# GpSimd's operations behind attention go to VectorE, and the planner gets new costs

## The chip, the cores and the metric

One core of a Trainium2 chip runs the whole program in one launch. The engines are TensorE (PE, matmuls; PEld is its weight load), VectorE (DVE), ScalarE (ACT), GpSimd (POOL) and SyncE (SP, which issues the DMAs). The metric is the device time of one execution in microseconds. The kernel before took 591.49 us, the median of three runs (590.26 to 592.46).

## The reference

Three stages follow one another. The first is a decayed linear attention over 2 batches, 8 heads, 768 tokens and 64 columns per head, in blocks with a running state; its output is one matrix of 1536 tokens x 512. Two feed-forward layers follow, 512 to 2048 to 512:

```python
x = attn_out.transpose(0, 2, 1, 3).reshape(B * S, H * D)        # 1536 x 512
h = x @ w_in;  g = where(h > 0, h, exp(min(h, 0)) - 1);  x = g @ w_out       # layer 0, ELU
h = x @ w_in2; g = maximum(h, 0) + log1p(exp(-abs(h)));  y = g @ w_out2      # layer 1, softplus
```

All data is float32.

## The kernel before, in words

**Numbers in two parts.** Each float32 matrix is split into a high part (rounded by ScalarE to the matmul's format) and a low part (value minus high part, a `tensor_tensor` subtract). A product is three matmuls: high x high, high x low, low x high (L387 to L389 for `x @ w_in`, L437 for `g @ w_out`). All large matmuls have 512 columns.

**Tiles.** The 1536 tokens are three tiles t = 0, 1, 2 of 512. The 2048 hidden columns of a layer are 16 blocks c of 128. A key (layer, t, c) is one block of hidden values for one tile: 12 matmuls into a PSUM bank (`hps`), the activation on ScalarE and VectorE, a split into g (high on ScalarE, L777, low by `minus`, L545), and 12 matmuls into the four accumulators y0 to y3. When a run of keys of one tile (a unit) ends, the four accumulators are taken out to `yacc` (L1094 and L1096 copy, L1099 adds), and the next unit's y matmuls wait for that.

**PLAN.** "one" runs a block for tile 0, "two" a pair of blocks for tiles 1 and 2, and "fast" (layer 0 only, seven pairs) does a pair of blocks for tiles 1 and 2 with 7 half products instead of 8; in exchange it needs sums and differences of blocks of x (`first_sums`, L996 on, tiles `sums`, t1 to t4) and of weights (`sum_ops`, L830 on, tiles `sumsw`, s0 and s1). These are elementwise operations between SBUF tiles; `minus` is L545, `plus` L548. The products go to PSUM tiles pa, pb and pd; `copy_op` (L936 ScalarE, L938 VectorE) and `add_op` (L945) combine them. ELU ends in L450; softplus ends in L758 (s5), `minus` (s6) and L764 (s7), which also gives the PSUM bank back. There are four such banks (b0 to b3).

**Weights** arrive as 64-bit words; ScalarE (L628, L632) and VectorE (L637, L642) make floats of them, ScalarE the high part (L647), `minus` the low one. SP loads them.

**The order.** Attention with the first eight blocks is written out by hand (`start`, `early_step`), with GpSimd doing some of it (L273, L279, L377, L1282). Everything behind it is made of `Op` objects in `build()`: `on` says on which engines an operation may run and what it is thought to cost, `key` is its due time, `after` its predecessors. `schedule()` plays this through at build time: whenever an engine falls free in the plan, it takes the ready operation with the earliest due time, and that emits the instruction. On the chip each engine then runs its own list strictly in order. An operation that may run on either engine (`both`, `half`) goes to the one that the plan finds free first; V_LO, W_LO, W_SUM, W_HALF, W_SLO, T_LO, T_SUM and SOFT are such. The plan's costs are MM3 for three matmuls, SCALAR for ScalarE, TT_V and TT_G for an operation with all operands in SBUF on VectorE and GpSimd, PS_V for one that reads PSUM; `both and pool[0] > now` stretches a VectorE operation that the plan sees beside a GpSimd one. PE picks between y matmuls (`m2_seq`) and products (`m1_seq`); at PILE = 2 ready keys the y matmuls come first.

**The end.** The last unit's four accumulators are added, stored by SP in four DMAs, and `probe()` (L1223) runs 15 matmuls into a free bank.

Of the kernel before, what the change touches and what calls it, by code (L numbers as in the profile page):

```python
# [55 lines left out]
def body(ctx, tc, lamc, attqk, attkv, w1, w2, out):  # L56
# [398 lines left out]
    order = count()  # L455

    class Op:

        def __init__(self, on, key, fn, after=(), gate=None, end=None):
            self.on, self.key, self.fn, self.gate, self.done = on, key, fn, gate, end  # L460
            self.then, self.wait, self.n, self.gone, self.first = [], 0, next(order), False, False
            self.behind(*after)
            ops.append(self)
# [7 lines left out]
    def schedule(pe, free):  # L471
# [3 lines left out]
        heads = [0] * len(pe)  # L475
        pool = [0.0]

# [6 lines left out]
        def begin(op, e):  # L484
            op.gone = True
            took = op.on[e]
            if e == "V" and isinstance(took, tuple):
                took, both = took
                if both and pool[0] > now:
                    over = pool[0] - now  # L490
                    took = over + took - SHARE * over if SHARE * over < took else took / SHARE
            if e == "G":
                pool[0] = now + took
            op.fn(e) if len(op.on) > 1 else op.fn()
            busy, late = took if isinstance(took, tuple) else (took, took)
            free[e] = now + busy
            heappush(events, (free[e], next(seen), None))
            heappush(events, (now + late + 0.06, next(seen), op))
# [5 lines left out]
        while left:  # L504
            now, _, op = heappop(events)
            if op is not None:
                left -= 1
                if op.done:
                    op.done()
                for nxt in op.then:  # L510
                    nxt.wait -= 1
                    if nxt.wait == 0:
                        enter(nxt)
            if events and events[0][0] <= now:
                continue
            if free["P"] <= now:
                m2_seq, m1_seq = pe
                ahead = list(takewhile(lambda o: o.wait == 0, m2_seq[heads[0]:heads[0] + 8]))
                can = [bool(ahead), heads[1] < len(m1_seq) and m1_seq[heads[1]].wait == 0]
                can[1] = can[1] and (m1_seq[heads[1]].gate is None or m1_seq[heads[1]].gate())  # L520
                if can[0] and (not can[1] or sum(o.on["P"] > MM3 for o in ahead) + sum(o.on["P"] == MM3 for o in ahead) // 4 >= PILE and not m1_seq[heads[1]].first):
                    pick = 0
                else:
                    pick = 1 if can[1] else None
                if pick is not None:
                    heads[pick] += 1
                    begin(pe[pick][heads[pick] - 1], "P")
            for e in "SAGV":
                if free[e] > now:
                    continue  # L530
                ready[e] = [x for x in ready[e] if not x[2].gone]
                for x in ready[e]:
                    if x[2].gate is None or x[2].gate():
                        begin(x[2], e)
                        break
            if not events and left:
                raise RuntimeError(f"stuck: {left}, {[(q[h].key, q[h].wait) for q, h in zip(pe, heads) if h < len(q)]}")
        return now


    MM3, SCALAR, TT_V, TT_G, PS_V = 0.68, 0.65, (0.71, True), 1.4, (0.71, False)
    SHARE, PILE = 0.35, 2

# [6 lines left out]
    engines = {"V": V, "G": G}  # L550
    both = {"G": TT_G, "V": TT_V}
    half = {"G": 0.76, "V": (0.42, True)}
    wide = {"G": 2.7, "V": (1.28, True)}

    def build():
# [54 lines left out]
        def weights_ops():  # L610
            for k, task in enumerate(tasks):
# [45 lines left out]
                o2 = Op({"A": SCALAR}, key, a2, [o1, summed_[t1] if t1 else None])  # L657
                o3 = Op({"V": 0.55}, key, v1, [o1])
                o4 = Op({"V": 0.75}, key, v2, [o3, o2])
                o5 = Op({"A": SCALAR}, key, a3, [o4])  # L660
                o6 = Op(W_LO, key, v3, [o5])
                loads[task] = ld, o2
# [40 lines left out]
        for key in queue[EARLY - 2:]:  # L703
            pos = nom["m2", key]
            if begins(key) or ends(key):
                parts = [Op({"P": MM3}, pos + m * MM3, lambda key=key, m=m: m2_part(key, m)) for m in range(KD)]
            else:
                parts = [Op({"P": 4 * MM3}, pos, lambda key=key: m2(key))]
            m2_ops[key], m2_last[key] = parts, parts[-1]
            m2_seq.extend(parts)  # L710
            for p in parts:
                p.behind(need(("o", key[0] * NF + key[2])))

        def act_ops(key, src, after, done):

# [3 lines left out]
            if layer == 0:  # L719
# [12 lines left out]
                o = Op({"A": SCALAR}, k, x2, [o])  # L732
                o = Op({"V": PS_V}, k, x3, [o], end=done)
            else:
# [33 lines left out]
                o = Op({"A": SCALAR}, k, s2, [o])  # L768
                o = Op(PLUS_ONE, k, s3, [o])
                o4 = Op({"A": SCALAR}, k, s4, [o])  # L770
                o5 = Op({"V": PS_V}, k, s5, [o4])
                o6 = Op(SOFT, k, s6, [o5], end=lambda: eu.append(box["i"]))
                o = Op({"V": PS_V}, k, s7, [o6], end=done)

# [9 lines left out]
            h = Op({"A": SCALAR}, k, hi, [o, m2_last.get(queue[j - 3])])  # L784
            low = Op(V_LO, k, lo, [h], end=lambda: vfree.add(box["k"]))
            for p in m2_ops[key]:
# [43 lines left out]
        def sum_ops(q):  # L830
# [26 lines left out]

            o0 = Op(W_SUM, k0, g0, deps)
            o1 = Op(W_HALF, k0, g1, deps)
            o2 = Op(W_HALF, k0, g2, deps)  # L860
            o3 = Op(W_HALF, k0, lambda e: plus(e, cut(0), cut(3), cut(0)), [o1, o2])
            o4 = Op(W_HALF, k1, lambda e: minus(e, cut(3), cut(1), cut(3)), [o0, o3])
            o5 = Op(W_HALF, k0, lambda e: minus(e, cut(1), cut(0), cut(1)), [o4])
            o6 = Op(W_HALF, k1, lambda e: minus(e, cut(2), cut(2), cut(1)), [o5])
            out_ = []
            for i, key, deps in ((0, k0, [o5, o3]), (1, k1, [o6, o4])):
# [9 lines left out]
                h = Op({"A": SCALAR}, key, hi, deps + held.get(("s", i), []))  # L876
                out_.append(Op(W_SLO, key, lo, [h]))
            held["sums_r"] = out_
# [4 lines left out]
        def quick(layer, p):  # L883
# [47 lines left out]
            def copy_op(src, tag, key, after):  # L931
# [7 lines left out]

                return Op(COPY, key, fn, after + held.get(tag, []))  # L940

# [23 lines left out]
            held["s", 0], held["s", 1] = [p5, p6], [p3, p7]  # L965
            held["p1"] = [act_ops(keys[0, 1], lambda: box["p1"], [a11], None)]
            held["u2"] = [act_ops(keys[0, 2], lambda: box["u2"], [a12], None)]
            held["p5"] = [act_ops(keys[1, 2], lambda: box["p5"], [a22], None)]
            act_ops(keys[1, 1], lambda: box["a"], [p4], lambda: give_bank(box["a"]))
# [12 lines left out]
        def part_ops(i, k, f, key, deps, new):  # L982
# [10 lines left out]
            h = Op({"A": SCALAR}, key, hi, deps)  # L993
            return h, Op(T_LO, key, lo, [h])

        def first_sums(plain_end):  # L996
# [10 lines left out]
            def chain(name, key, deps, *terms):  # L1007
                o = None
                for i, (fn, a, b) in enumerate(terms):

                    def go(e, i=i, fn=fn, a=a, b=b):
                        fn(e, box[name], a() if a else box[name], b())

                    o = Op(T_SUM, key, go, deps if o is None else [o])
                return o
# [61 lines left out]
        def unit_ops(u):  # L1077
# [8 lines left out]
            for m in range(KD):  # L1086
# [15 lines left out]
                if fresh:  # L1102
# [3 lines left out]
                    if layer == 0 and t == 2:  # L1106
                        deps += [gone["i", 0], gone["i", 1]]
                o = Op(COPY if fresh else {"V": PS_V}, key, fn, deps)
                mine.append(o)
# [14 lines left out]
        def split_ops(t):  # L1124
# [4 lines left out]
            for m in range(KD):  # L1129
# [10 lines left out]
                prev = h if m == 0 else prev  # L1140
                xdone[1, t].append(Op(V_LO, key0 + m * MM3 - 3.0, lo, [h]))
            held["acc", t] = list(xdone[1, t])


# [12 lines left out]
        def close_units(keys_done):  # L1157
            while made_units[0] < len(units) and all(k in keys_done or queue.index(k) < EARLY for k in units[made_units[0]]):
# [4 lines left out]
                if t in ysplit and (1, t) not in xdone:  # L1163
                    split_ops(t)

# [35 lines left out]
    NV = 9  # L1201
    W_LO = both
    V_LO = both
    W_SUM, W_HALF, W_SLO = both, half, both
    T_LO, T_SUM = both, both
    SOFT = both
    PLUS_ONE = {"A": SCALAR}
# [3 lines left out]
    def close_attention():  # L1211
# [3 lines left out]
        late["tp"] = ctx.enter_context(tc.tile_pool(name="ltp", bufs=1, reuse_waits="tile"))  # L1215

    def probe():
        ps = pp.tile([P, TT], F32, tag="b0", name="probe")
        a, x = halves["i", 2 * NF - 1][0][:, 0:P], xh[0][0]
        b = x.rearrange("p a n -> p (a n)")  # L1220
        for n in (256, 384, 512):
            for i in range(5):
                T.matmul(ps[:, :n], a, b[:, :n], start=True, stop=True, skip_group_check=True)  # L1223

# [72 lines left out]
    with tc.manual_schedule():  # L1297
# [4 lines left out]
        build()  # L1302
        probe()

# [45 lines left out]
```

## Time and profile before

| | |
|---|---|
| median of three runs | 591.49 us |
| the profiled execution | 590.46 us |
| its span, first to last instruction | 588.7 us |
| mean granted clock of TensorE | 0.994 |
| PE busy | 573.4 us (97%) |
| DVE busy | 414.9 us (70%) |
| ACT busy | 368.4 us (63%) |
| POOL busy | 316.7 us (54%) |

Shares are of the span. A matmul is recorded from its start to its modelled end, and matmuls overlap, so PE's speed is read from the distance of their starts. The list of waits says how long an engine stood idle and whose work ended the wait. A granted clock of 1 is 2.4 GHz, of 0.5 it is 1.2 GHz.

### The profile page before, as it was taken

How to read it: one execution, taken by the hardware profiler on the slowest of the kernel's cores; microseconds unless marked ns; L12 is line 12 of the kernel's file. 1: busy time of each engine (PE TensorE's matmuls, PEld its weight loads, DVE VectorE, ACT ScalarE, POOL GpSimd, SP SyncE). 2: the span in 40 equal slices, each digit the busy share in tenths (PEclk: the TensorE clock that was granted, in tenths of full speed). 3: DMA queues.
4: the chain of work that ended last, by engine and by line, in shares of the span. 5: the costliest groups of instructions: out<-in, count | busy, mean ns of one | idle time of the engine just before them, and what ended most of it. 6: DMA issues, size and time to landing. Idle time of an engine off the chain costs nothing.

```text
span 588.7 us, 8054 instructions
## 1 busy us (share of the span) xinstructions
PE 573.4 (97%) x2999; PEld 467.9 (79%) x2999; DVE 414.9 (70%) x546; ACT 368.4 (63%) x652; POOL 316.7 (54%) x246
## 2 busy tenths in 40 slices
PE   8899999979999989999999999999999999999999
PEld 7777778757788878888888788887888887888887
DVE  6678778999868398845887937687785479633732
ACT  1365657647876667645868568887794488464720
POOL 4634356998755374544374835547453555343541
PEclk9999999989999999999999999999999999999999
DMA  8944642101214122420223102132223011000023
GB/s 317 409 165 126 243 157 90 37 0 36 73 45 135 38 70 72 144 72 1 84 96 107 37 1 72 36 108 71 73 71 108 1 37 36 1 0 1 0 85 130
DMA packets 14582, 49.80 MB, mean 85 GB/s; under 512 B 1744, under 2 KB 1744, under 8 KB 14544
## 3 DMA queue, kind: packets, MB, share of 16 engines
q1 hardware_dynamic: 14544, 49.30, 24.3%
q8 instruction: 23, 0.38, 0.3%
q14 instruction: 15, 0.12, 0.1%
HBM read 46.14 MB, written 3.15 MB: 84 GB/s over the span
## 4 chain that ended last, share of the span: by engine, by line
PE 63%; DVE 20%; ACT 5%; DMA 5%; POOL 3%; issue 3%; SPq 0%; DVEq 0%; ACTq 0%
PE y L437 31%; PE hps L387 8%; PE hps L388 8%; PE hps L389 8%; DMA raw<-w 4%; DVE r L164 2%; PE pa L387 2%; PE pa L389 2%; PE pa L388 2%; DVE sums L545 2%; DVE u L758 2%; DVE v L450 2%; DVE r L642 2%; DVE r L637 2%; DVE yacc L1099 1%
## 5 line engine op out<-in xcount | busy, mean ns | idle before, releaser
L545 POOL TENSOR_TENSOR g<-v,g 128x512 fp32r<-128x512 f32 x69 | 96.1, 1393 | 98.2 <-ACT g L777 98.2
L437 PE MATMUL y<-g,woh 128*128 128x512 f32 x384 | 119.4, 392 | 0.8 <-ACT yacc L1094 0.8
L437 PE MATMUL y<-woh,g 128*128 128x512 f32 x384 | 118.2, 389 | 0.0
L777 ACT ACTIVATE g<-v 128x512 fp32r<-128x512 f32 x89 | 56.1, 631 | 73.7 <-PE y L437 68.6
L545 POOL TENSOR_TENSOR v<-v,u 128x512 f32<-128x512 f32 x38 | 52.9, 1392 | 61.7 <-DVE u L758 61.7
L437 PEld LDWEIGHTS y<-g,woh 128*128 128x128 f32 x384 | 71.6, 188 | 17.1 <-ACT yacc L1094 1.6
L437 PEld LDWEIGHTS y<-woh,g 128*128 128x128 f32 x384 | 72.1, 188 | 14.9
L387 PE MATMUL hps<-xh,wih 128*128 128x512 f32 x200 | 79.6, 398 | 0.8 <-DVE v L764 0.6
L388 PE MATMUL hps<-xl,wih 128*128 128x512 f32 x200 | 78.3, 391 | 0.4 <-POOL xl L545 0.4
L389 PE MATMUL hps<-xh,wil 128*128 128x512 f32 x200 | 78.1, 391 | 0.0
L437 PE MATMUL y<-g,wol 128*128 128x512 f32 x192 | 74.8, 389 | 0.0
L437 PE MATMUL y<-wol,g 128*128 128x512 f32 x192 | 74.7, 389 | 0.0
L1099 DVE TENSOR_TENSOR yacc<-y,yacc 128x512 f32<-128x512 f32 x68 | 45.4, 687 | 35.9 <-PE y L437 35.8
L758 DVE SCALAR_TENSOR_TENSOR u<-u,e 128x512 f32<-128x512 f32 x48 | 43.6, 908 | 32.4 <-ACT v L754 32.4
L642 DVE CUSTOM_DVE_ANT_0 r<-r,c 128x1024 uint16<-128x1024 uint16 x49 | 46.8, 956 | 6.7 <-ACT c L632 6.1
L387 PEld LDWEIGHTS hps<-xh,wih 128*128 128x128 f32 x200 | 37.8, 189 | 11.8 <-DVE v L764 2.7
L764 DVE SCALAR_TENSOR_TENSOR v<-hps,v 128x512 f32<-128x512 f32 x48 | 32.8, 684 | 18.2 <-POOL v L545 18.0
L388 PEld LDWEIGHTS hps<-xl,wih 128*128 128x128 f32 x200 | 37.8, 189 | 8.2 <-POOL xl L545 0.8
L389 PEld LDWEIGHTS hps<-xh,wil 128*128 128x128 f32 x200 | 37.7, 188 | 7.9
L437 PEld LDWEIGHTS y<-wol,g 128*128 128x128 f32 x192 | 36.0, 188 | 7.5
L437 PEld LDWEIGHTS y<-g,wol 128*128 128x128 f32 x192 | 36.0, 188 | 7.5
L741 ACT ACTIVATE e<-hps 128x512 f32<-128x512 f32 x48 | 28.2, 587 | 16.0 <-PE hps L389 15.0
(198 smaller groups left out, 1158.4 us busy)
## 6 DMA issues: line engine op xcount, KB each, us to landing
raw<-w SPq DMA_DIRECT2D x64, 512.0 KB, 3.7
qk<-attqk SPq DMA_DIRECT2D x8, 512.0 KB, 7.0
kv<-attkv SPq DMA_DIRECT2D x8, 512.0 KB, 7.0
out<-yacc SPq DMA_DIRECT2D x12, 256.0 KB, 2.1
early<-attkv SPq DMA_DIRECT2D x2, 512.0 KB, 9.2
early<-attqk SPq DMA_DIRECT2D x2, 512.0 KB, 10.6
earlykv<-attkv SPq DMA_DIRECT2D x2, 512.0 KB, 10.9
earlyqk<-attqk SPq DMA_DIRECT2D x2, 512.0 KB, 10.9
```

Of the source, the lines that this page charges most:

```text
L164: V.tensor_tensor(out=ri, in0=ri, in1=c, op=ALU.add)
L387: T.matmul(ps, wh[:, wo[i]], xa[i], start=(start and i == 0), stop=False, skip_group_check=True)
L388: T.matmul(ps, wh[:, wo[i]], xb[i], start=False, stop=False, skip_group_check=True)
L389: T.matmul(ps, wl[:, wo[i]], xa[i], start=False, stop=(stop and i == n - 1), skip_group_check=True)
L437: T.matmul(yps[m], a, b, start=(begins(key) and i == 0), stop=(ends(key) and i == 2))
L545: engines[e].tensor_tensor(out=o, in0=a, in1=b, op=ALU.subtract)
L642: V.tensor_tensor(out=ri, in0=ri, in1=box["c"], op=ALU.add)
L741: A.activation(out=box["e"], in_=src(), func=AF.Abs)
L758: V.scalar_tensor_tensor(out=u, in0=u, scalar=-1.0, in1=box["e"], op0=ALU.add, op1=ALU.subtract)
L764: V.scalar_tensor_tensor(out=box["v"], in0=src(), scalar=0.0, in1=box["v"], op0=ALU.max, op1=ALU.add)
L777: A.activation(out=g[:, 0], in_=box["v"], func=AF.Copy)
L1099: V.tensor_tensor(out=y, in0=yps[m], in1=y, op=ALU.add)
```

## The change

Every group that could go to either engine behind attention now has only VectorE in its dictionary. An operation that takes its engine as an argument is made by `Either`, since the number of engines no longer tells. In the planner's model, VectorE and GpSimd operations whose operands are all in SBUF would hold a common port one after the other (`port`); a GpSimd operation would start only with QUEUE ready ones waiting for VectorE; but no operation has GpSimd in its dictionary. New costs: VectorE 0.69 us (half size 0.415), ScalarE 0.635, and `PIPE`: the engine falls free that much before the result is there. The activation of keys of the fast pairs whose value lies in SBUF is marked as such (`bank=False`). The count of ready y matmuls is now a sum of their costs. `second_sums()` is the counterpart of `first_sums` for layer 1; it is called only where FAST[1] is true, and it is false. `probe()` and its call are gone. The hand-written attention part is as before.

```diff
+    def Either(on, key, fn, after=(), gate=None, end=None):
+        return Op(on, key, fn, after, gate, end, True)
...
-        pool = [0.0]
+        port = {"V": 0.0, "G": 0.0}
...
             took = op.on[e]
-            if e == "V" and isinstance(took, tuple):
-                took, both = took
-                if both and pool[0] > now:
-                    over = pool[0] - now
-                    took = over + took - SHARE * over if SHARE * over < took else took / SHARE
-            if e == "G":
-                pool[0] = now + took
-            op.fn(e) if len(op.on) > 1 else op.fn()
-            busy, late = took if isinstance(took, tuple) else (took, took)
+            op.fn(e) if op.names else op.fn()
+            if e in "VG":
+                took, shared = took
+                if shared:
+                    took += max(0.0, port["VG"[e == "V"]] - now - 0.14)
+                    port[e] = now + took
+            busy, late = took if isinstance(took, tuple) else (took - PIPE[e], took)
...
-                if can[0] and (not can[1] or sum(o.on["P"] > MM3 for o in ahead) + sum(o.on["P"] == MM3 for o in ahead) // 4 >= PILE and not m1_seq[heads[1]].first):
+                if can[0] and (not can[1] or sum(o.on["P"][0] for o in ahead) / (4 * MM3) >= PILE and not m1_seq[heads[1]].first):
...
+                if e == "G" and sum(not x[2].gone for x in ready["V"]) < QUEUE:
+                    continue
...
-    MM3, SCALAR, TT_V, TT_G, PS_V = 0.68, 0.65, (0.71, True), 1.4, (0.71, False)
-    SHARE, PILE = 0.35, 2
+    MM3, SCALAR, SB_V, SB_G, PS_V = 0.68, 0.635, (0.69, True), (1.295, True), (0.69, False)
+    PIPE = {"P": 0.0, "A": 0.1, "V": 0.08, "G": 0.04, "S": 0.0}
+    PILE, QUEUE = 2, 3
...
-                o3 = Op({"V": 0.55}, key, v1, [o1])
-                o4 = Op({"V": 0.75}, key, v2, [o3, o2])
+                o3 = Op({"V": (0.42, True)}, key, v1, [o1])
+                o4 = Op({"V": SB_V}, key, v2, [o3, o2])
                 o5 = Op({"A": SCALAR}, key, a3, [o4])
-                o6 = Op(W_LO, key, v3, [o5])
+                o6 = Either(W_LO, key, v3, [o5])
...
-    W_LO = both
-    V_LO = both
-    W_SUM, W_HALF, W_SLO = both, half, both
-    T_LO, T_SUM = both, both
-    SOFT = both
+    W_LO = {"V": SB_V}
+    V_LO = {"V": SB_V}
+    W_SUM, W_HALF, W_SLO = {"V": SB_V}, {"V": half["V"]}, {"V": SB_V}
+    T_LO, T_SUM = {"V": SB_V}, {"V": SB_V}
+    SOFT = {"V": SB_V}
     PLUS_ONE = {"A": SCALAR}
     COPY = {"A": SCALAR, "V": PS_V}
...
-    def probe():
-        ps = pp.tile([P, TT], F32, tag="b0", name="probe")
-        a, x = halves["i", 2 * NF - 1][0][:, 0:P], xh[0][0]
-        b = x.rearrange("p a n -> p (a n)")
-        for n in (256, 384, 512):
-            for i in range(5):
-                T.matmul(ps[:, :n], a, b[:, :n], start=True, stop=True, skip_group_check=True)
...
         build()
-        probe()
```

## Rows read from the trace of the kernel before

**Rows 1.** Windows: stretch, length, then busy us and count by engine, clock, DMA

```profile
95.20:584.90 489.70, 480.65 (x2098) 393.18 (x2097) 344.85 (x427) 320.51 (x567) 274.02 (x204) 1.00 0.17 56
...
93.40:124.80 31.40, 27.16 (x118) 21.50 (x116) 30.05 (x26) 17.80 (x33) 30.11 (x21) 1.00 0.14 46
93.40:159.90 66.50, 60.40 (x254) 47.88 (x253) 62.59 (x66) 43.65 (x79) 59.09 (x45) 0.97 0.14 46
204.90:216.90 12.00, 11.05 (x49) 8.82 (x47) 11.76 (x14) 7.34 (x14) 9.63 (x10) 1.00 0.30 107
126.30:129.70 3.40, 3.40 (x9) 2.63 (x9) 3.40 (x5) 1.54 (x3) 3.40 (x3) 0.51 0.00 0
```

**Rows 2.** Chain that ended last: start us, us, what, how many

```profile
554.29 30.60 PE y L437 x135
```

**Rows 3.** PE's waits from 100 us on: us in total, times, longest

```profile
PE pd L387 <- DVE v L450: 4.2, 1, 4.2
PE pa L387 <- DVE p L938: 1.7, 1, 1.7
PE pa L387 <- DVE p L945: 1.1, 2, 0.9
PE y L437 <- ACT yacc L1094: 0.8, 1, 0.8
PE hps L387 <- DVE v L764: 0.8, 2, 0.6
PE hps L388 <- POOL xl L545: 0.4, 1, 0.4
```

**Rows 4.** Timeline of PE behind its longest pause: start us, us, what

```profile
126.47 0.63 PE L387 MATMUL pd<-t1h,s0h 128*128 128x512 f32 x1
126.90 0.63 PE L388 MATMUL pd<-t1l,s0h 128*128 128x512 f32 x1
```

**Rows 5.** Timeline of DVE, the operation that ended the pause

```profile
124.81 0.68 DVE L450 SCALAR_TENSOR_TENSOR v<-v,hps 128x512 f32<-128x512 f32 x1
```

**Rows 6.** Timelines of DVE and POOL, working beside each other

```profile
118.07 1.77 DVE L545 TENSOR_TENSOR sums<-sums,xl2a 128x512 f32<-128x512 f32 x1
119.77 1.78 DVE L545 TENSOR_TENSOR sums<-xh,sums 128x512 f32<-128x512 f32 x1
...
117.56 1.74 POOL L545 TENSOR_TENSOR s1l<-sumsw,s1h 128x512 fp32r<-128x512 f32 x1
```

**Rows 7.** Timeline of DVE with POOL idle beside it

```profile
99.66 0.68 DVE L548 TENSOR_TENSOR sums<-sums,xl2a 128x512 f32<-128x512 f32 x1
100.26 0.68 DVE L545 TENSOR_TENSOR sums<-sums,xl 128x512 f32<-128x512 f32 x1
...
162.23 0.41 DVE L545 TENSOR_TENSOR sumsw<-sumsw 128x256 f32<-128x256 f32 x1
162.56 0.68 DVE L450 SCALAR_TENSOR_TENSOR v<-v,p 128x512 f32<-128x512 f32 x1
```

**Rows 8.** Timeline of ACT, a wait in front of the first evictions

```profile
116.50 0.63 ACT L870 ACTIVATE s1h<-sumsw 128x512 fp32r<-128x512 f32 x1 [1.05 <-DVE sumsw L545]
```

**Rows 9.** Groups by line: count, busy us, mean ns, idle before, releaser

```profile
L545 POOL TENSOR_TENSOR g<-v,g 128x512 fp32r<-128x512 f32 x69 | 96.1, 1393 | 98.2 <-ACT g L777 98.2
...
L1099 DVE TENSOR_TENSOR yacc<-y,yacc 128x512 f32<-128x512 f32 x68 | 45.4, 687 | 35.9 <-PE y L437 35.8
...
L1096 DVE COPY yacc<-y 128x512 f32<-128x512 f32 x11 | 7.6, 690 | 1.9 <-PE y L437 1.7
L1094 ACT ACTIVATE yacc<-y 128x512 f32<-128x512 f32 x13 | 7.5, 593 | 9.7 <-PE y L437 9.7
```

**Rows 10.** The end: chain, DMA issues by SP, and DMA landing times

```profile
584.89 2.62 PE probe L1223 x15
...
561.84 24.13 SPq L1114 DMA_DIRECT2D out<-yacc  x12
...
out<-yacc SPq DMA_DIRECT2D x12, 256.0 KB, 2.1
```

More of the change, by code (lines that the diff above doesn't have):

```diff
@@ L455, in body, with __init__ @@
     order = count()
+    def Either(on, key, fn, after=(), gate=None, end=None):
+        return Op(on, key, fn, after, gate, end, True)
     class Op:
-        def __init__(self, on, key, fn, after=(), gate=None, end=None):
+        def __init__(self, on, key, fn, after=(), gate=None, end=None, names=False):
             self.on, self.key, self.fn, self.gate, self.done = on, key, fn, gate, end
             self.then, self.wait, self.n, self.gone, self.first = [], 0, next(order), False, False
+            self.names = names
             self.behind(*after)
@@ L550, in body @@
     engines = {"V": V, "G": G}
-    both = {"G": TT_G, "V": TT_V}
-    half = {"G": 0.76, "V": (0.42, True)}
-    wide = {"G": 2.7, "V": (1.28, True)}
+    both = {"V": SB_V, "G": SB_G}
+    half = {"V": (0.415, True), "G": (0.74, True)}
     def build():
@@ L705, in build @@
             if begins(key) or ends(key):
-                parts = [Op({"P": MM3}, pos + m * MM3, lambda key=key, m=m: m2_part(key, m)) for m in range(KD)]
+                parts = [Op({"P": (MM3, MM3 + 0.17)}, pos + m * MM3, lambda key=key, m=m: m2_part(key, m)) for m in range(KD)]
             else:
-                parts = [Op({"P": 4 * MM3}, pos, lambda key=key: m2(key))]
+                parts = [Op({"P": (4 * MM3, 4 * MM3 + 0.17)}, pos, lambda key=key: m2(key))]
             m2_ops[key], m2_last[key] = parts, parts[-1]
@@ L712, in build, with act_ops @@
                 p.behind(need(("o", key[0] * NF + key[2])))
-        def act_ops(key, src, after, done):
+        def act_ops(key, src, after, done, bank=True):
             layer, t, c = key
@@ L732, in act_ops @@
                 o = Op({"A": SCALAR}, k, x2, [o])
-                o = Op({"V": PS_V}, k, x3, [o], end=done)
+                o = Op({"V": PS_V if bank else SB_V}, k, x3, [o], end=done)
             else:
@@ L768, in act_ops @@
                 o = Op({"A": SCALAR}, k, s2, [o])
-                o = Op(PLUS_ONE, k, s3, [o])
+                o = Either(PLUS_ONE, k, s3, [o])
                 o4 = Op({"A": SCALAR}, k, s4, [o])
-                o5 = Op({"V": PS_V}, k, s5, [o4])
-                o6 = Op(SOFT, k, s6, [o5], end=lambda: eu.append(box["i"]))
-                o = Op({"V": PS_V}, k, s7, [o6], end=done)
+                o5 = Op({"V": SB_V}, k, s5, [o4])
+                o6 = Either(SOFT, k, s6, [o5], end=lambda: eu.append(box["i"]))
+                o = Op({"V": PS_V if bank else SB_V}, k, s7, [o6], end=done)
             def hi():
@@ L784, in act_ops @@
             h = Op({"A": SCALAR}, k, hi, [o, m2_last.get(queue[j - 3])])
-            low = Op(V_LO, k, lo, [h], end=lambda: vfree.add(box["k"]))
+            low = Either(V_LO, k, lo, [h], end=lambda: vfree.add(box["k"]))
             for p in m2_ops[key]:
@@ L856, in g2 @@
                 plus(e, cut(0), f32(halves[tb][0][:, HALF:DM]), f32(halves[tb][1][:, HALF:DM]))
[L858 to L864, printed above, removed]
+            o0 = Either(W_SUM, k0, g0, deps)
+            o1 = Either(W_HALF, k0, g1, deps)
+            o2 = Either(W_HALF, k0, g2, deps)
+            o3 = Either(W_HALF, k0, lambda e: plus(e, cut(0), cut(3), cut(0)), [o1, o2])
+            o4 = Either(W_HALF, k1, lambda e: minus(e, cut(3), cut(1), cut(3)), [o0, o3])
+            o5 = Either(W_HALF, k0, lambda e: minus(e, cut(1), cut(0), cut(1)), [o4])
+            o6 = Either(W_HALF, k1, lambda e: minus(e, cut(2), cut(2), cut(1)), [o5])
             out_ = []
@@ L876, in sum_ops @@
                 h = Op({"A": SCALAR}, key, hi, deps + held.get(("s", i), []))
-                out_.append(Op(W_SLO, key, lo, [h]))
+                out_.append(Either(W_SLO, key, lo, [h]))
             held["sums_r"] = out_
@@ L938, in fn @@
                         V.tensor_copy(h, box[src])
-                return Op(COPY, key, fn, after + held.get(tag, []))
+                return Either(COPY, key, fn, after + held.get(tag, []))
             def add_op(tag, src, key, after, done=None):
@@ L965, in quick @@
             held["s", 0], held["s", 1] = [p5, p6], [p3, p7]
-            held["p1"] = [act_ops(keys[0, 1], lambda: box["p1"], [a11], None)]
-            held["u2"] = [act_ops(keys[0, 2], lambda: box["u2"], [a12], None)]
-            held["p5"] = [act_ops(keys[1, 2], lambda: box["p5"], [a22], None)]
+            held["p1"] = [act_ops(keys[0, 1], lambda: box["p1"], [a11], None, False)]
+            held["u2"] = [act_ops(keys[0, 2], lambda: box["u2"], [a12], None, False)]
+            held["p5"] = [act_ops(keys[1, 2], lambda: box["p5"], [a22], None, False)]
             act_ops(keys[1, 1], lambda: box["a"], [p4], lambda: give_bank(box["a"]))
@@ L993, in part_ops @@
             h = Op({"A": SCALAR}, key, hi, deps)
-            return h, Op(T_LO, key, lo, [h])
+            return h, Either(T_LO, key, lo, [h])
         def first_sums(plain_end):
@@ L1012, in go @@
                         fn(e, box[name], a() if a else box[name], b())
-                    o = Op(T_SUM, key, go, deps if o is None else [o])
+                    o = Either(T_SUM, key, go, deps if o is None else [o])
                 return o
@@ L1107, in unit_ops @@
                         deps += [gone["i", 0], gone["i", 1]]
-                o = Op(COPY if fresh else {"V": PS_V}, key, fn, deps)
+                o = Either(COPY if fresh else {"V": PS_V}, key, fn, deps)
                 mine.append(o)
@@ L1140, in split_ops, with second_sums, keep, hi @@
                 prev = h if m == 0 else prev
-                xdone[1, t].append(Op(V_LO, key0 + m * MM3 - 3.0, lo, [h]))
+                xdone[1, t].append(Either(V_LO, key0 + m * MM3 - 3.0, lo, [h]))
             held["acc", t] = list(xdone[1, t])
+        def second_sums():
+            p = next(p for kind, layer, p in PLAN if kind == "fast" and layer == 1)
+            pos = [nom[1, p, "P", k] - 3.0 for k in range(7)]
+            y = {(t, m): o for t in (1, 2) for m, o in enumerate(ysplit[t])}
+            clear = xuse[1] + xuse[2]
+            done = {i: [] for i in (1, 2, 3, 4)}
+            xdone[1, 1], xdone[1, 2] = [None] * KD, [None] * KD
+            made_x = {}
+            reads = {1: [], 2: []}
+            tmp = {}
+            prior = {}
+            def keep(t, m, key):
+                def hi():
+                    if t not in made_x:
+                        made_x[t] = True
+                        new_x(t, 1)
+                    A.activation(out=xh[t][m // 2][:, m % 2], in_=yacc[0, t][m], func=AF.Copy)
+                def lo(e):
+                    minus(e, xl[t][m // 2][:, m % 2], yacc[0, t][m], f32(xh[t][m // 2][:, m % 2]))
+                h = Op({"A": SCALAR}, key, hi, [y[t, m]] + clear)
+                o = Either(V_LO, key, lo, [h])
+                xdone[1, t][m] = o
+                reads[t].append(o)
+                return o
+            def sub(key, out_, a, b, deps):
+                return Either(V_LO, key, lambda e: minus(e, out_(), a(), b()), deps)
+            def yy(t, m):
+                return lambda: yacc[0, t][m]
+            for i in range(2):
+                def tmp_new(i=i):
+                    tmp[i] = late["hp"].tile([P, TT], F32, tag=("p1", "p5")[i], name="sums3")
+                k11 = keep(1, i, pos[0])
+                k21 = keep(1, 2 + i, pos[1])
+                k22 = keep(2, 2 + i, pos[3])
+                def t3(e, i=i, tmp_new=tmp_new):
+                    tmp_new()
+                    minus(e, tmp[i], yacc[0, 2][2 + i], yacc[0, 2][i])
+                f3 = Either(V_LO, pos[2], t3, [y[2, i], y[2, 2 + i]] + held.get(("p1", "p5")[i], []))
+                f1 = sub(pos[2], yy(2, i), yy(2, i), yy(1, i), [f3, y[1, i]])
+                f2 = sub(pos[3], yy(2, 2 + i), yy(2, 2 + i), yy(2, i), [f1, k22])
+                f4 = sub(pos[6], yy(1, 2 + i), yy(1, 2 + i), yy(2, 2 + i), [f2, k21])
+                for n, f, o in ((1, yy(2, i), f1), (2, yy(2, 2 + i), f2), (3, lambda i=i: tmp[i], f3), (4, yy(1, 2 + i), f4)):
+                    h, low = part_ops(n, i, f, pos[{1: 2, 2: 3, 3: 5, 4: 6}[n]], [o, prior.get(n)] + clear, i == 0)
+                    prior[n] = h
+                    done[n].append(low)
+                    if n == 3:
+                        held[("p1", "p5")[i]] = [low]
+                reads[2] += [f1, f2, done[1][-1], done[2][-1], f3]
+                reads[1] += [f1, f4, done[4][-1]]
+                reads[2] += [f4]
+            held["acc", 1], held["acc", 2] = reads[1], reads[2]
+            tdone[1] = done
@@ L1163, in close_units @@
                 if t in ysplit and (1, t) not in xdone:
-                    split_ops(t)
+                    if t == 0 or not FAST[1]:
+                        split_ops(t)
+                    elif t == 1:
+                        second_sums()
         keys_done = {k for k in queue[:EARLY]}
```

## Prediction

> **What bounds the kernel now.** I read the stretches first, by windows: from the end of the attention part to the last y matmul TensorE (PE) is busy 480.7 of 489.7 us, VectorE (DVE) 344.9, GpSimd (POOL) 274.0 [rows 1]. So a microsecond is won only where PE stands still or runs slowly. Next, how much that is: in the chain of work 135 matmuls behind one another take 30.60 us, 0.2267 us each [rows 2]; the stretch has 2098 of them [rows 1], and 2098 x 0.2267 = 475.6. About 14.1 us are lost, the most that the change can win. The list of PE's waits names 9.0 of them [rows 3]; the largest, 4.2 us, is one wait of pd for a DVE operation of L450. The timeline of PE shows the price behind it: after that pause the matmuls start 0.43 us apart [rows 4], and the granted clock of that stretch is 0.51, the 1.2 GHz level [rows 1]. Eight such steps cost 8 x 0.20 = 1.6 us. The rest, some 3.5 us, is slips of 0.1 to 0.3 us.
>
> Why was L450 as late as 124.81 [rows 5]? Before it DVE and POOL worked on the block sums side by side, and the reader should see how: DVE starts at 118.07 and 119.77, 1.70 us apart, one POOL operation beside each, and all of them are recorded at over 1.7 us [rows 6]. Where nothing of POOL's runs beside it, a 128x512 operation of DVE lets the next start after 0.60 us (99.66, 100.26) and a 128x256 one after 0.33 (162.23, 162.56) [rows 7]; below I take 0.605 and 0.335. So a lockstep pair of large ones costs 1.70 us, and the same two on DVE alone 1.21: this is the whole argument for the change.
>
> **The change part by part.** *All of POOL's work behind attention to DVE.* From 95.2 to 584.9 DVE has 427 operations and POOL 204 [rows 1]. At 0.605 us each (the half-size ones too, an upper price) 631 take 382 us of 489.7, 78%. DVE's busy time now is 344.9, although its own 427 cost at most 258 alone: the lockstep stretches them by 87 us, and that is given back. DVE has room over the whole; the question is the places.
>
> *The first sums, 93.4 to 124.8.* DVE has 26 operations there, POOL 21 [rows 1]; one of each had begun before. 45 x 0.605 = 27.2 us; nine are of half size (as the short one in [rows 7]), which takes 9 x 0.27 off: 24.8. In the same order L450 would start at 93.4 + 24.8 to 27.2 = 118.2 to 120.6 instead of 124.81: 4.2 to 6.6 us earlier. The wait was 4.2, so it goes (-4.2), and with it the slow clock behind it (-1.6). The 0.8 us wait for yacc on ScalarE [rows 3] lies in the same stretch: ScalarE's queue stood behind a 1.05 us wait for a sumsw of DVE [rows 8], which falls earlier with the rest (-0.8). What is late next: pd needs a free bank, the t1 and the s12 halves; all three are in the count.
>
> *The second knot, 204.9 to 216.9.* PE waits 1.7 us for a copy of L938 [rows 3]. DVE had 14 operations, POOL 10, in the 12 us [rows 1]: 24 x 0.605 = 14.5 at the upper price; with seven half-size ones, and without the three at the edges, which need not be done first, 21 x 0.605 - 7 x 0.27 = 10.8. That is 1.2 us earlier than now or, at the upper price, 2.5 later. The half-size price is the measured one; I take -1.0.
>
> *Layer 2.* Waits of 0.8 us in two places for L764, and 0.4 for an xl of POOL [rows 3]. The operations ahead of them are stretched ones; bounds 0 and -1.2, I take -0.8. The 1.1 us for p of L945 stay: the matmul needs an addition that needs the matmul before it.
>
> *Low part of g.* It ran on POOL 69 times, 1393 ns on the mean [rows 9]; on DVE alone an operation of this size is done in 0.7 [rows 7]. The chain from ScalarE's high part to the y matmul gets 0.7 us shorter wherever DVE is free. PE has other matmuls ready then: 0.
>
> *New waits.* DVE's queue runs in order, so what POOL did beside it now stands in front of something. The tightest stage is 93.4 to 159.9: 66 and 45 operations [rows 1], two of them begun before; 109 x 0.605 = 65.9, with 29 half-size ones 58.1, for a stage that would shrink from 66.5 to 59.9 us (-4.2 - 1.6 - 0.8). That is 97% or more of it. Weight preparation, which is not urgent, can move past the stage; bounds of the loss 0 and the whole 6.6, I take +1.0, nearer to 0 because the lateness that was measured already has these operations in it.
>
> *The schedule's new costs.* DVE 0.69 with the next start 0.08 earlier, ScalarE 0.635 with 0.1 earlier, are for DVE what the rows show [rows 7]; before, it planned 0.71 without overlap and shared stretches of another form. This alters the order in ways that no row gives: bounds -3.5 (all slips gone) and +3.5, I take 0. Names, the unused second_sums and the evened count of ready matmuls: 0.
>
> *The probe.* Its 15 matmuls are done by 584.89 + 2.62 = 587.5; the last store is issued by 585.97 and stores land in 2.1 us [rows 10], about 587.7, behind which the end of the program stands. It is hidden by the store: 0 (at most -0.2 if not).
>
> Sum: -4.2 - 1.6 - 0.8 - 1.0 - 0.8 + 1.0 = -7.4 us. The profiled execution took 590.46 us (its span 588.7 and 1.8 around it); so 583.1. The median of the runs shown is 591.49, 1.0 above it, and against that the same sum gives 584.1. I predict 584.0.
>
> **Where a page speaks.** Evictions of y (L1099) read one operand from PSUM and take 687 ns on the mean [rows 9], while operations with both operands in SBUF were stretched to 1.7 [rows 6]: POOL's 274 us did not touch them. The Trainium skill, "SBUF — State Buffer", section "Who interferes with whom", says so as a rule: a VectorE instruction with at most one SBUF input, outside the two-port modes, does not contend with GpSimd. The trace agrees. By that rule POOL's work beside such operations was free help, and the change turns it into a queue ahead of them; that is the third rival below, whose price comes from rows alone.
>
> **Rivals.**
> 1. *All slips go too.* DVE is rid of stretched operations everywhere, and the plan's costs fit: nearly all 14.1 us vanish, 591.5 - 13 = 578. For it: DVE's 78%. Against it: the additions between dependent matmuls (1.1 us), and slips that hang on PE and ScalarE alone.
> 2. *DVE becomes the bound of the sums' stage.* At 97% of the shortened stage a single wrong order stops PE, the pause moves to another matmul and the slow clock comes with it: of the -6.6 some 2 remain, with -1.8 elsewhere and +1 there: 591.5 - 2.8 = 588.7. For it: the upper price, 65.9 us, doesn't fit into 59.9. Against it: weight preparation in that count can wait.
> 3. *Slower: the change of accumulators.* The 68, 11 and 13 evictions [rows 9] make 92, four to a unit, so 23 units and 22 changes at which the next unit's y matmuls wait for an eviction. Each moved operation ahead of the first eviction costs 0.605 us there if PE has nothing else: 22 x 0.605 = 13.3 us for one, so 591.5 - 8.4 + 13.3 = 596.4. It decides from 8.4/13.3 = 0.63 uncovered operations per change on. For it: a low part of g is often due just then. Against it: PE's waits name an eviction once, 0.8 us [rows 3], DVE idled 35.9 us in front of evictions [rows 9], and a first-layer product of 2.7 us often lies between.
>
> **How the numbers follow.** Forecast 0.59, rival 1 0.11, rival 2 0.17, rival 3 0.13. What a measurement can tell from no change is about 0.5%, 588.5 to 594.4. The forecast's own range is 580.5 to 587.5 and rival 1 lies below; with 0.05 of rival 2 that is faster 0.75. The other 0.12 of rival 2 are the same, rival 3 is slower 0.13. For 8 in 10 the range takes rival 1's middle and rival 2: 578 to 591.
>
> **What would show it.** Right: no POOL row behind attention; 128x512 DVE operations at 0.69 us or less throughout; the 4.2 us wait of pd and the low clock behind it gone; DVE busy about 360 us from 95 to the end. Wrong: a PE wait of over 2 us between 110 and 160 on DVE (rival 2), or waits of y for yacc at many units, 10 us in sum (rival 3).

## The result, and the profile after

The changed kernel takes 581.89 us (median of four runs, 581.46 to 583.23) against 591.3 beside it: 0.9844 of the time before, interval 0.982 to 0.9869. Predicted were 584.0 us, a range of 578 to 591, and faster at 0.75. The profiled execution took 581.46 us, its span is 579.7 us, 9.0 less than before.

The page's busy line of the changed kernel, and its windows (columns as in [rows 1]; the last stretch is the one behind TensorE's longest pause):

```profile
PE 566.3 (98%) x2984; PEld 465.7 (80%) x2984; DVE 442.9 (76%) x745; ACT 371.1 (64%) x658; POOL 40.8 (7%) x41
```

```profile
95.20:576.00 480.80, 476.92 (x2102) 393.81 (x2100) 372.16 (x630) 324.20 (x575) 0.00 (x0) 1.00 0.18 58
93.40:124.80 31.40, 28.92 (x135) 23.52 (x130) 30.11 (x54) 20.09 (x36) 1.31 (x1) 1.00 0.15 51
93.40:159.90 66.50, 63.23 (x284) 51.60 (x279) 64.45 (x120) 48.18 (x87) 1.31 (x1) 1.00 0.15 48
204.90:216.90 12.00, 12.00 (x55) 9.94 (x54) 11.82 (x24) 10.01 (x19) 0.00 (x0) 1.00 0.28 95
124.40:127.80 3.40, 3.40 (x17) 2.79 (x16) 3.40 (x8) 2.25 (x5) 0.00 (x0) 1.00 0.00 0
```

VectorE does 630 operations in the stretch where it did 427 beside GpSimd's 204 [rows 1], and is busy only 27 us more. From 93.4 to 124.8 us it gets through 54, where both engines together had 47. Its operations are no longer stretched, as the groups by line show (count, busy us, mean ns, idle before):

```profile
L550 DVE TENSOR_TENSOR g<-v,g 128x512 fp32r<-128x512 f32 x89 | 61.0, 687 | 27.2 <-ACT g L781 26.7
L1103 DVE TENSOR_TENSOR yacc<-y,yacc 128x512 f32<-128x512 f32 x68 | 45.3, 688 | 30.7 <-PE y L437 30.6
```

The low part of g takes half of GpSimd's 1393 ns [rows 9]; the eviction, which reads PSUM, takes 688 where it took 687 before: that one was never stretched. TensorE's waits behind attention, in place of the six of [rows 3]:

```profile
PE pd L387 <- DVE v L450: 2.5, 1, 2.5
PE pa L387 <- DVE p L949: 0.8, 1, 0.8
```

9.0 us of named waits have become 3.3. Summing, from 92 us on, what the starts of PE's matmuls lie further apart than 0.2267 us gives 14.4 us before and 3.9 after: 10.5 us won. Of the 14.4, 9.3 lie up to 160 us and 5.1 behind it; of the 3.9, all lie up to 160 us. The span shows 9.0 of the 10.5, because the attention part, which the change leaves alone, ended 1.3 us later in this execution (over the fourteen profiles of this study its end varies by about 3 us).

The largest wait is still the one for L450. The timeline of VectorE from the first operation behind the attention part to this L450:

```profile
95.86 0.67 DVE L553 TENSOR_TENSOR sumsw<-wih,wil 128x512 f32<-128x512 f32 x1
96.46 0.68 DVE L550 TENSOR_TENSOR sums<-xh2a,xh 128x512 f32<-128x512 f32 x1
...
121.83 0.68 DVE L550 TENSOR_TENSOR t4l<-sums,t4h 128x512 fp32r<-128x512 f32 x1
122.43 0.68 DVE L553 TENSOR_TENSOR sums<-sums,xl 128x512 f32<-128x512 f32 x1
123.03 1.28 DVE L450 SCALAR_TENSOR_TENSOR v<-v,hps 128x512 f32<-128x512 f32 x2
```

Its row of before is [rows 5], at 124.81. VectorE now starts a large operation every 0.60 us, with 0.6 us of idle time in all, but all the sums, those of t3 and t4 too, which PE needs later, stand ahead of the L450 that frees the bank.

### The profile page after: what moved, and what is told of

It is laid out like the page before. It is cut to its first block, busy times and chain, and to the rows that moved or that the text cites. A ratio compares the mean times of both kernels' runs of the same rounds, so it can differ in the third digit from the quotient of the medians.

```text
span 579.7 us, 7908 instructions
## 1 busy us (share of the span) xinstructions
PE 566.3 (98%) x2984; PEld 465.7 (80%) x2984; DVE 442.9 (76%) x745; ACT 371.1 (64%) x658; POOL 40.8 (7%) x41
## 4 chain that ended last, share of the span: by engine, by line
PE 83%; DVE 9%; DMA 5%; ACT 2%; issue 1%; SPq 0%; DVEq 0%; ACTq 0%
PE y L437 42%; PE hps L387 10%; PE hps L389 10%; PE hps L388 10%; DMA raw<-w 4%; PE pa L387 2%; PE pa L389 2%; PE pa L388 2%; DVE r L164 1%; DMA kv<-attkv 1%; DVE sc L309 1%; PE pd L389 1%; PE pd L387 1%; PE pd L388 1%; DVE r L162 1%; DVE v L450 1%
## 5 line engine op out<-in xcount | busy, mean ns | idle before, releaser
L550 DVE TENSOR_TENSOR g<-v,g 128x512 fp32r<-128x512 f32 x89 | 61.0, 687 | 27.2 <-ACT g L781 26.7
L1103 DVE TENSOR_TENSOR yacc<-y,yacc 128x512 f32<-128x512 f32 x68 | 45.3, 688 | 30.7 <-PE y L437 30.6
L762 DVE SCALAR_TENSOR_TENSOR u<-u,e 128x512 f32<-128x512 f32 x48 | 33.0, 688 | 19.2 <-ACT v L758 18.6
L646 DVE CUSTOM_DVE_ANT_0 r<-r,c 128x1024 uint16<-128x1024 uint16 x49 | 33.6, 685 | 4.0 <-ACT c L636 3.4
L632 ACT ACTIVATE r<-raw 128x512 f32<-128x512 f32 x49 | 32.5, 663 | 2.4 <-DMA raw<-w 1.9
L550 DVE TENSOR_TENSOR v<-v,u 128x512 f32<-128x512 f32 x48 | 33.1, 689 | 1.0
```

What stands on the lines that cost most here:

```text
L550: engines[e].tensor_tensor(out=o, in0=a, in1=b, op=ALU.subtract)
L632: A.activation(out=r, in_=high.bitcast(F32), func=AF.Prelu, scale=2.0 ** -112, alpha=-2.0 ** 32)
L646: V.tensor_tensor(out=ri, in0=ri, in1=box["c"], op=ALU.add)
L762: V.scalar_tensor_tensor(out=u, in0=u, scalar=-1.0, in1=box["e"], op0=ALU.add, op1=ALU.subtract)
L1103: V.tensor_tensor(out=y, in0=yps[m], in1=y, op=ALU.add)
```

## The experiments

Medians and ratios are against the kernel before on the same chip. The experiments ran on four chips (a to d, e to h, i to k, and l), so kernels of one group compare best; c, which differs from the changed kernel by the probe alone, stands for it among a to d. "Sums" is the time from the first operation on `sums` to the end of the last low part of t4, in the one profiled execution, read from groups by tile as shown below the table. "Pause" is PE's longest wait behind attention.

| kernel | us | ratio, interval | sums | pause |
|---|---|---|---|---|
| changed kernel | 581.89 | 0.9844 (0.982 to 0.9869) | 28.4 | 2.5 |
| a: both engines, new costs | 585.59 | 0.9889 (0.9868 to 0.991) | 35.6 | 5.2 |
| b: VectorE alone, old costs | 585.58 | 0.9883 (0.9852 to 0.9914) | 30.5 | 4.9 |
| c: changed, with the probe | 581.97 | 0.9828 (0.9798 to 0.9858) | 28.4 | 2.5 |
| d: changed, L450 due earlier | 578.93 | 0.9775 (0.9758 to 0.9792) | 30.3 | 1.2 |
| e: before, L450 due earlier | 591.74 | 1.0006 (0.9984 to 1.0028) | 36.0 | 3.4 |
| f: b, L450 due earlier | 581.49 | 0.9824 (0.9783 to 0.9865) | 33.2 | 2.7 |
| g: a, L450 due earlier | 587.43 | 0.9929 (0.9905 to 0.9953) | 36.9 | 5.6 |
| h: g with QUEUE 3 | 587.99 | 0.9934 (0.9916 to 0.9953) | 36.9 | 5.6 |
| i: d, copies due earlier | 579.62 | 0.9804 (0.9783 to 0.9825) | 30.3 | 1.2 |
| j: g, copies due earlier | 587.6 | 0.9931 (0.9912 to 0.9949) | 37.2 | 5.5 |
| k: i, softplus part on GpSimd | 579.91 | 0.9806 (0.9786 to 0.9826) | 30.3 | 1.2 |
| l: i, t3 in other buffers | 578.4 | 0.9765 (0.9743 to 0.9787) | 29.6 | 0.9 |

Before, the sums took 35.5 us. The groups by tile behind that column (min, median and max ns, then first and last start), for the changed kernel and for a:

```profile
L550 DVE TENSOR_TENSOR sums<-xh2a,xh x2: 676/676/676, 96.5 to 99.2; 128x512 f32<-128x512 f32 x2
...
L550 DVE TENSOR_TENSOR t4l<-sums,t4h x2: 680/680/681, 121.8 to 124.2; 128x512 fp32r<-128x512 f32 x2
```

```profile
L550 POOL TENSOR_TENSOR sums<-xh2a,xh x2: 1472/1473/1474, 95.6 to 97.0; 128x512 f32<-128x512 f32 x2
...
L550 DVE TENSOR_TENSOR t4l<-sums,t4h x1: 1472/1472/1472, 129.7 to 129.7; 128x512 fp32r<-128x512 f32 x1
```

**a: the engines alone undone.**

```diff
-    PILE, QUEUE = 2, 3
+    PILE, QUEUE = 2, 0
...
-    V_LO = {"V": SB_V}            # and the seven groups beside it
+    V_LO = both
```

> The changed kernel with both engines in the dictionaries again and QUEUE 0, so that GpSimd takes some 190 operations as before; the new costs and the model of the common port stay. Theory (the gain is the lockstep's): VectorE operations beside GpSimd are stretched to 1.7 us again, the pause of TensorE in the sums' stage is 4 us or more, 588 to 593 us. Rival (the gain is the planner's new costs): 581 to 584 us.

Measured: 585.59 us, between the two. Its waits of PE:

```profile
PE pd L387 <- DVE v L450: 5.2, 1, 5.2
PE pa L387 <- DVE p L949: 0.8, 1, 0.8
PE y L437 <- DVE yacc L1103: 0.4, 1, 0.4
```

The stretched operations and the large pause are back, as the theory said, and the sums take 35.6 us again. But the waits of the second knot and of layer 1, 2.9 us of [rows 3], are gone but for 0.4, although GpSimd works beside VectorE there. The planner's new costs and rules did that without the change of engines.

**b: the engines alone changed.** The kernel before with VectorE alone in the dictionaries, by the old cost TT_V.

```diff
-    V_LO = both
+    VO = {"V": TT_V}
+    V_LO = VO                     # and the other groups likewise
```

> The kernel before with only its dictionaries changed: VectorE alone behind attention, old costs and old rules, probe kept. Theory (lockstep): most of the gain is there, 581 to 585 us. Rival (new costs): under a third of the gain, 588 us or more.

Measured: 585.58 us, just beyond the theory's bound; two thirds of the gain (6.8 of the 10.4 us that c won on the same chip). Its waits:

```profile
PE pd L387 <- DVE v L450: 4.9, 1, 4.9
PE pa L387 <- DVE p L946: 1.0, 1, 1.0
```

Again the later waits are gone, this time without the new costs; but the pause is longer than before, 4.9 us, though nothing stretches VectorE. From the end of the attention part to the late L450 VectorE had 46 operations with 3.3 us of idle time between them (the changed kernel 47 with 0.6). The sums are done in 30.5 us instead of 35.5, and TensorE gains little by it, as L450 stands behind them. The excess of TensorE's starts shows where each half works. Up to 160 us it was 9.3 us before, and is 8.7 in a, 8.2 in b and 5.6 in c; behind 160 us it was 5.1, and is 0.9, 0.0 and 0.0. So the sums' stage needs both halves of the change, while for the later stages either one is nearly enough; that is why 1.2% and 1.1% make 1.6% together and not 2.3%.

**c: the probe back.**

> The changed kernel with the 15 probe matmuls behind it. Theory: hidden by the last store, 0 to 0.3 us longer than the changed kernel, 581.9 to 582.2 us. Rival: they were on the path, 2.6 us longer, 584.5 us.

Measured: 581.97 us, nothing to tell from the changed kernel. Chain and store issues of its end:

```profile
578.04 2.62 PE probe L1297 x15
...
576.76 2.37 SPq L1118 DMA_DIRECT2D out<-yacc  x4
```

The probe ends at 580.66. The issue of the last store begins at 578.80 (and ends at 579.13), and the store lands 2.1 us after that beginning, at 580.88. So the store hides the probe, by 0.2 us. This run showed something else. The instructions around the pause are those of the changed kernel, the pause is 2.5 us in both, but here the stretch behind it ran at a low clock (the window below is 0.54; in the changed kernel's profile the same window has 1.00, and so has the one shown above):

```profile
126.30:129.70 3.40, 3.40 (x10) 2.59 (x9) 2.76 (x7) 1.54 (x3) 0.00 (x0) 0.54 0.00 0
```

**d: the bank's end sets L450's due time.**

```diff
-                o = Op({"V": PS_V if bank else SB_V}, k, x3, [o], end=done)
+                due = min(k, nom[key] + 4 * MM3 + 3.0) if key in nom else k
+                o = Op({"V": PS_V if bank else SB_V}, due, x3, [o], end=done)
```

> The changed kernel with an earlier due time for the L450 operation of keys whose product is in a PSUM bank: the bank's end, not the y matmul, sets it. Theory (the 2.5 us pause that is left is an order of due times: VectorE does t2 to t4 sums before the L450 that frees the bank): the pause goes and 2 to 3 us with it, 579 to 580 us. Rival (VectorE is full in the sums' stage and the pause only moves): 581 to 583 us, with a PE wait of 2 us or more for t3 or t4 instead.

Measured: 578.93 us, at the fast end of what the theory said. The wait of pd is gone; what is left:

```profile
PE pa L387 <- ACT p L941: 1.2, 1, 1.2
PE pa L387 <- DVE p L950: 1.1, 1, 1.1
```

So the wait for L450 that the change left was an order of due times. About half of it came back as a wait for the copy of pa, which l explains: the named waits fell from 3.3 to 2.3 us, less than the 3.0 us between the medians of c and d. The rest is probably the low clock, which d's profile does not have: the mean clock of d's four runs is 0.995 to 0.997, that of three of c's four 0.994, as in c's profile with its slow stretch.

**e, f, g, h: the same edit elsewhere.** e is the kernel before, f is b, g is a, h is a with the changed kernel's QUEUE 3, each with d's edit.

> The kernel before with nothing but the earlier due time for the L450 operation of keys whose product is in a PSUM bank. Theory (the 4.2 us pause was an order of due times, on either division of work): the wait of pd and the slow clock behind it go, 5 to 6 us, 586 to 587 us. Rival (the pause was the lockstep's price, VectorE and GpSimd together were too late with the sums): the pause only moves to t1, t2 or t3, 590 us or more.

Measured: 591.74 us, no gain; the theory fell. Its longest waits:

```profile
PE pa L387 <- ACT p L937: 3.4, 1, 3.4
PE pa L387 <- DVE p L946: 2.8, 2, 1.6
PE pa L387 <- DVE p L939: 1.7, 1, 1.7
```

The bank is free in time, and PE now waits for the copy of pa, which ScalarE runs behind t3 and t4. With both engines the sums end too late in this order too, as in g and j below.

> VectorE alone with the old costs, plus the earlier due time. Theory (in the first experiments the two halves of the change differed from the whole only by this pause and the slow clock): 578.5 to 580 us, within 1 us of the changed kernel with the same edit (578.9). Rival (the old costs also order the rest worse): 581 us or more.

Measured: 581.49 us, beyond the theory and inside the rival's bound. In the profiled execution (580.53 us) the low clock is gone, a pause of 2.7 us for the copy of pa remains, and the sums take 33.2 us, 3 more than in d. Only the planner's costs and rules differ (and the probe, which c shows to be hidden), so the old ones order the sums worse; by the time the two are not told apart for certain, as their intervals overlap a little (0.9783 to 0.9865 and 0.9758 to 0.9792).

> Both engines with the new costs and QUEUE 0, plus the earlier due time. Theory (lockstep costs only where the work is dense, and that is the sums' stage): VectorE operations stay stretched, but with the pause gone 579 to 581 us. Rival (lockstep itself delays the sums): a pause of 2 us or more for t2, t3 or t4 takes the place, 582 us or more.

Measured: 587.43 us; the rival was right in the time and in the pause, which is 5.6 us, but for the copy of pa and not for a t itself.

> Both engines with the new costs and the changed kernel's QUEUE 3 (GpSimd starts one only with three ready for VectorE), plus the earlier due time. Theory: as VectorE has room, GpSimd's help brings nothing, 578.5 to 581 us, not below VectorE alone (578.9). Rival (help at the dense places pays): 577.5 us or less.

Measured: 587.99 us, neither. GpSimd took 65 operations only, 41 of them before 160 us, where VectorE had most to do, and the sums took as long as in g, where it took 214. Help where the work is dense costs 9 us against d.

**i and j: copies due earlier.** `copy_op` k1, k5, k2 and the addition a22 get earlier keys, in d and in g.

```diff
-            k1 = copy_op("a", "p1", pos[3] - 1.0, [p1])
+            k1 = copy_op("a", "p1", pos[1], [p1])
```

> The changed kernel with the earlier due time for L450 and earlier due times for the three copies and the addition between the half products (k1, k5, k2, a22). Theory (VectorE alone ends the sums by 125, so what is left is order): the 1.2 us wait of pa for a copy goes, some of the 1.1 us wait for an addition too; 576.5 to 578 us. Rival (the sums themselves are too late): the wait moves to t3 or t4, 578.5 us or more.

Measured: 579.62 us, with the same 1.2 us for the same copy; the theory fell, and the rival's wait for t3 or t4 did not come either. The reason stands in the code: t3's sums lie in the buffers p1 and p5 until they have been split, and the copy of pa goes to p1, so no due time can bring it ahead of them.

> The same due times with both engines (QUEUE 0). Theory (lockstep: the sums' stage takes 35 to 37 us with both engines, 28 to 30 with VectorE alone, in whatever order): TensorE now waits for t3 or t4 themselves, 5 us or more with the slow clock, 584 to 587 us. Rival (the rest of the difference was order): 580 us or less.

Measured: 587.6 us, some 0.6 beyond the theory's bound and far from the rival. The wait is still the copy's, which passes on the end of t3:

```profile
PE pa L387 <- ACT p L941: 5.5, 1, 5.5
PE pa L387 <- DVE p L950: 0.8, 1, 0.8
```

Against i, which differs only in who may do the work, it is 8.0 us slower.

**k: lockstep where there is room.** i with `SOFT = {"G": SB_G}` and QUEUE 0.

> The first kernel of this set with layer 1's 48 softplus subtractions (s6) fixed on GpSimd, none elsewhere. Theory (lockstep costs time only where VectorE is full; in layer 1 it has room): VectorE operations of layer 1 are stretched again, the time stays within 1 us of the kernel without it. Rival (any GpSimd work beside VectorE costs): 2 us or more.

Measured: 579.91 us, within 0.3 us of i: the theory held. VectorE's groups from 300 us on, in k and then in i:

```profile
L550 DVE TENSOR_TENSOR g<-v,g 128x512 fp32r<-128x512 f32 x52 | 42.7, 822 | 18.5 <-ACT g L782 18.4
...
L646 DVE CUSTOM_DVE_ANT_0 r<-r,c 128x1024 uint16<-128x1024 uint16 x23 | 21.8, 947 | 4.4 <-ACT c L636 4.0
```

```profile
L550 DVE TENSOR_TENSOR g<-v,g 128x512 fp32r<-128x512 f32 x52 | 35.9, 690 | 15.6 <-ACT g L782 15.3
...
L646 DVE CUSTOM_DVE_ANT_0 r<-r,c 128x1024 uint16<-128x1024 uint16 x22 | 15.2, 689 | 2.5 <-ACT c L636 2.2
```

The low part of g is stretched from 690 to 822 ns on the mean and the weights' addition (L646) from 689 to 947, and TensorE does not notice.

**l: t3 out of the shared buffers.**

```diff
-                        box["f3", k] = late["hp"].tile([P, TT], F32, tag=("p1", "p5")[k], name="sums3")
+                        box["f3", k] = late["tp"].tile([P, TT], F32, tag=f"e{k}", name="sums3")
...
-            held["p1"], held["p5"] = read3, read3
```

> The kernel with the earlier due times, and the t3 sums no longer in the buffers p1 and p5 that the copies of pa and pd need, but in two buffers that only layer 1 uses. Theory (the earlier due times brought nothing since the copy of pa must wait until t3 has left its buffer, so the 1.2 us wait is the end of the sums, passed on by a shared buffer): the copy runs some 10 us earlier, the 1.2 us wait goes, y matmuls fill the place of the 1.0 us wait too, 577 to 578.5 us. Rival (VectorE is full there, the wait only moves on to t3 or t4): 579 us or more.

Measured: 578.4 us. The copy of pa runs at 111.15 us (in i at 122.24), and of the waits one is left:

```profile
PE pa L387 <- DVE p L950: 0.9, 1, 0.9
```

The excess of PE's starts is 1.2 us, of 14.4 before. This is the fastest kernel here, ahead of the changed one by 0.8% (0.9765 against 0.9844, intervals apart); against d (0.9775) and i (0.9804) the intervals overlap, so that l is faster than these is not shown by the time.

## Why the prediction was right, point by point

- **The mechanism** was right where it is measured by itself: with both engines the sums took 35.5 to 37.2 us in six kernels of different planner costs and orders, with VectorE alone 28.4 to 33.2. It was not GpSimd's own pace that VectorE waited for: VectorE was busy 30.1 of the 31.4 us before [rows 1], with 26 operations that at 0.605 us take 15.7. After the change VectorE was busy 372 us from 95.2 us on, where about 360 were forecast.
- **The wait of pd (-4.2)** is the step that failed, "in the same order L450 would start" 4.2 to 6.6 us earlier. It started 1.8 us earlier, at 123.03. The prices held: 40 large operations and 7 of half size, at 0.605 and 0.335 us, make 26.5 us, with 0.6 of idle time 27.1, and 27.2 were measured. The order did not. With one engine the due times put a sum and a low part of t4 and two evictions ahead of L450, four operations or 2.4 us that the count of 45 did not have, and the stage began 1.3 us later. So the 27.2 us agree with the forecast's upper price, which took 45 large operations, by chance. The wait fell to 2.5, so -1.7. That it stayed at 4.9 in b and left in d says what it hung on: the order, once the lockstep is gone. Before that the order was no use (e).
- **The low clock (-1.6)** was gone in the profiled execution; c shows that this was luck, the same pause had it again. The mean clock was 0.997 in this execution and 0.994, as in c's profile, in the other three of the changed kernel, so it was probably there in those.
- **The first evictions (-0.8)** came true: no wait for yacc is left.
- **The second knot (-1.0)** was 1.7: nothing waits there now. **Layer 2 (-0.8)** was all of the 1.2 named.
- **New waits (+1.0)**: none. At 97% VectorE was as full as worked out (64.5 of 66.5 us busy), and apart from L450 nobody waited for it longer than before.
- **The new costs (0)** were mis-sized: c, which has them, is 3.6 us faster than b, which has not, on the same chip. They let VectorE run the sums with 0.6 us of idle time instead of 3.3, and what they won lies up to 160 us (an excess of 8.2 in b, 5.6 in c).
- **The small slips**, some 3.5 us that the sum left standing, went but for some 0.6. This is where most of the 3 us beyond the sum came from (-10.5 for -7.4), and the new costs were not needed for it: behind 160 us b, with the old costs, has nothing left either.
- **The sum** came near in part by luck. Up to 160 us -5.6 were forecast (-4.2 - 1.6 - 0.8 + 1.0); the change of engines alone brought -1.1 there (9.3 to 8.2 in b), and it took the new costs, put at 0, to reach -5.4 (3.9 left; -3.7 with the low clock, as in c). Behind 160 us -1.8 were forecast and -5.1 came.
- **The probe (0)** held (c). **Rival 3**, evictions behind moved operations, did not appear at all: no wait for yacc. What the Trainium skill, "SBUF — State Buffer", section "Who interferes with whom", says of operations with at most one SBUF input outside the two-port modes, and the prediction drew on, agrees with the evictions' own time, 687 ns beside GpSimd and 688 without it. But VectorE had room in front of them, 30.7 us of idle time. **Rival 2** has its sign, a PE wait of over 2 us on VectorE between 110 and 160: there is one of 2.5, although the time is that of the forecast. **Rival 1**, that all slips go too, came true for the slips and not for the waits; its 578 us is what d and l reach.

What stays open: which of the new costs (VectorE's, ScalarE's, the overlap of starts) does the work in a; they were changed together only, with the planner's rules. Each kernel was profiled once, so the sums, waits and excess are those of one execution. And why either half suffices for the later stages was not taken apart.

## What to carry to other kernels

Two engines that hold each other up can be slower than the faster one alone (here 1.70 us for a pair, against 1.21), and the place to look is where both are full: with L450 in time, VectorE alone was 8.0 us faster than both (i and j), while in layer 1, with room and the new costs, it made no difference (k). That the work is done sooner is not enough: in b the sums took 5 us less, and TensorE's longest wait was no shorter (4.9 us, 4.2 before), for an operation queued behind them. When work changes engines, count the queue that it joins in the new order, not in the old one; what frees a buffer for someone else needs a due time of its own. When a pause does not move with a due time, look for a buffer that two stages share.

## What the runs showed of the hardware

GpSimd's operation with both inputs in SBUF, without VectorE beside it, in the timeline of GpSimd in the kernel before:

```profile
577.52 1.29 POOL L545 TENSOR_TENSOR g<-v,g 128x512 fp32r<-128x512 f32 x1 [1.43 <-ACT g L777]
```

With a VectorE operation beside it, the pair took 1.70 us in lockstep [rows 6]. That is less than the 1.89 us of the two alone (0.60 between starts on VectorE [rows 7] and this 1.29), so they overlap a little. Operations with one input are not all spared: the shift of the weights (L641), which reads one SBUF tile, took 423 ns on the mean in i and 579 in k, with GpSimd at work. And the granted clock after a pause is not set by the program alone: the same instructions with the same 2.5 us pause had 1.00 behind it in one profile and 0.54 in another.
